# Retention units: outputs moved to the step of a later unit's scores, units 3.67 instead of 3.75 steps apart

## The chip, the cores and the metric

The kernel runs on one NeuronCore of a Trainium2 chip. The metric is the device time of one execution in microseconds (us); lower is better. The engines are named as in the profile: PE is TensorE (PEld its weight loads), DVE is VectorE, ACT is ScalarE, POOL is GpSimd, SP is SyncE, whose queue issues nearly all DMAs.

## What is computed

Retention (attention without softmax, with a decay per head), then a feed-forward layer with the gate h·cos(h), then a second one that takes the maximum of three projections:

```python
scores = scale * np.matmul(q, k.transpose(0, 1, 3, 2))      # 8 batches, 8 heads, 576 positions, 64 features
gamma = 1.0 - 2.0 ** (-5.0 - np.arange(H))
Dmat = np.where(rel >= 0, gamma[:, None, None] ** rel[None], 0.0)
attn_out = np.matmul(scores * Dmat[None], v)
x = attn_out.transpose(0, 2, 1, 3).reshape(B * S, H * D)    # 4608 tokens, 512 features
h = x @ w_in                                                # 512 -> 2048
x = (h * np.cos(h)) @ w_out                                 # 2048 -> 512
h = np.maximum(np.maximum(x @ w1, x @ w2), x @ w3)          # 512 -> 768
out = h @ w_out2                                            # 768 -> 512
```

All of it is in fp32. In the feed-forward layers each operand is split into a high and a low fp32r part, and the matrices are multiplied with seven quarter products (a Strassen-like scheme) instead of eight.

## The kernel before

The 4608 tokens are nine blocks of 512. Retention works in **units**: one unit is one block and one pair of heads, so there are 36 units; unit n is pair n % 4 of block n // 4, and its tile in the order of the instructions is named u{block}_{pair} (unit 18 is u4_2, its scores are sc18, its outputs po18). A unit goes through these functions:

- `att_load` (L550): one DMA of 1 MB on SP brings q, k and v of the unit into a tile of the pool `wpool` (8 buffers, shared with weights and with arenas in which weights are split).
- `att_scale` (L562): POOL scales v by the decay, in place.
- `att_scores` (L570): PE computes the scores of four chunks of 128 tokens, for two heads, into two PSUM banks. Contraction is over 64 rows, so a matmul uses a tile of 64 rows by 128 columns of the array.
- `att_mask` (L580): DVE multiplies the scores by the causal mask into SBUF.
- `att_state` (L609) and `att_keep` (L594): chunk by chunk, PE adds k·v to the running state of the head pair (128 by 128; 64 by 128 for a chunk of 64 tokens), which stands in one PSUM bank, and ACT copies the state before each chunk.
- `att_out` (L630): PE computes the outputs into one PSUM bank: masked scores times v (L637, 128 by 64 tiles), then the kept states times q (L649, 64 by 64 tiles).
- `att_decay` (L653): DVE scales the outputs into the block's quarters of x.

From these quarters `build_in` (L741) makes the split operands of the first feed-forward layer (differences on POOL, high parts on ACT, low parts on DVE) and SP stores them. The first layer's products for the first half of w_in run on PE in the same stretch (`group_in`, L458; `product_in`, L403): 12 matmuls of 256 columns per product on full 128 by 128 tiles, 14 products per block of tokens. The copies out of PSUM (L464, L470, the seed copy L487) and the gate (L516 to L540) are ACT's and DVE's, and SP stores the gate's results. `background` (L237) brings in later weights: a raw load (L180) on SP, a widening on ACT (L186), a join on DVE (L192), a sum on POOL (L198).

The order of work is written by hand. There is a list of **steps**; a product ends with `tick()` (L155), which runs what is due in that step. `at(k, fn, turn)` puts fn into the step k from now. Within a step, what is marked `AHEAD` comes first (scores and outputs, so they stand on PE between two products), `INSIDE` (state updates) goes into the next product or behind it, and the rest comes last. Every engine runs its own instructions in the order in which they were written. The first eight units run ahead of the products; from unit 8 on the start of a unit, in steps, is

```python
    def start_of(n):
        return (15 * (n - NLEAD)) // 4
```

and `att_unit` (L673) puts scores at the start, the mask one step later, the state updates in steps 1 to 5, the outputs in step 5 and the decay in step 6. The load is written four steps ahead of the start.

Of the kernel before, what the change touches and what calls it, by code (L numbers as in the profile page):

```python
# [39 lines left out]
def chunks_of(j):  # L40

    t0 = j * NB
    cut = (-t0) % S
    segs = [(0, cut), (cut, NB)] if 0 < cut < NB else [(0, NB)]
    out = [(a, min(CH, e - a)) for s, e in segs for a in range(s, e, CH)]
    full = [c for c in out if c[1] == CH]
    short = [c for c in out if c[1] < CH]  # L50
    assert len(short) in (0, 2) and all(n == CH // 2 for _, n in short)
    order = full + short
    col = {a: sum(n for _, n in order[:i]) for i, (a, _) in enumerate(order)}
    return [(a, n, col[a], (t0 + a) % S) for a, n in out]
# [47 lines left out]
def retention_ffn(ctx: ExitStack, tc: tile.TileContext, att, w_in, w_out, w123, w_out2, cst, out):  # L102
# [13 lines left out]
    def x4(name, shape, dt=F32):  # L116
        return xpool.tile([128, *shape], dt, tag="x", name=name)

    def bank(name):
        return ps.tile([128, NB], F32, tag="b", name=name)  # L120
# [21 lines left out]
    AHEAD, INSIDE, AFTER, LATER = range(4)  # L142

    def at(n, fn, turn=LATER):
        agenda.setdefault(slot[0] + n, [[], [], [], []])[turn].append(fn)
# [401 lines left out]
    def order_of(n):  # L547
        return divmod(n, NPAIR)

    def att_load(n):  # L550
        j, hp = order_of(n)
        w = w14(f"u{j}_{hp}", F32)
        units[n] = {
            "qk": w[:, : 2 * NB].rearrange("p (a n) -> p a n", a=2),
            "kv": w[:, 2 * NB : 4 * NB].rearrange("p (a n) -> p a n", a=2),
            "ret": w[:, 4 * NB : 6 * NB].rearrange("p (a n) -> p a n", a=2),
            "um": w[:, 6 * NB :].rearrange("p (k n) -> p k n", n=CH),
            "kept": {},
        }
        nc.sync.dma_start(out=w[:, : 4 * NB], in_=att[j, hp])  # L560

    def att_scale(n):  # L562

        v = units[n]["kv"][:, 1].rearrange("p (s d) -> p s d", d=64)
        col = CTV + n * 8
        nc.gpsimd.tensor_tensor(
            out=v, in0=v, in1=cs[:, col : col + 8].unsqueeze(2).to_broadcast([128, 8, 64]), op=ALU.mult
        )

    def att_scores(n):  # L570
        u = units[n]
        qT, kT = u["qk"][:, 0], u["qk"][:, 1]
        u["sc"] = [bank(f"sc{n}_{e}") for e in range(2)]
        for s in range(NB // CH):
            sl = slice(s * CH, (s + 1) * CH)
            for e in range(2):
                r = slice(64 * e, 64 * e + 64)
                nc.tensor.matmul(u["sc"][e][:, sl], kT[r, sl], qT[r, sl], start=True, stop=True)  # L578

    def att_mask(n):  # L580
        u = units[n]
        nfull = sum(m == CH for _, m, _, _ in chunks_of(order_of(n)[0]))
        for e in range(2):
            for at_, k, col in ((0, nfull, CM), (nfull, NB // CH - nfull, CM2)):
                if k:
                    sl = slice(at_ * CH, (at_ + k) * CH)
                    nc.vector.tensor_tensor(  # L587
                        out=u["ret"][:, e, sl].rearrange("p (s i) -> p s i", i=CH),
                        in0=u["sc"][e][:, sl].rearrange("p (s i) -> p s i", i=CH),
                        in1=cs[:, col : col + CH].unsqueeze(1).to_broadcast([128, k, CH]),  # L590
                        op=ALU.mult,
                    )

    def att_keep(n, i):  # L594

        u = units[n]
        j, hp = order_of(n)
        ch = chunks_of(j)
        if i >= len(ch):
            return  # L600
        _, m, _, pos = ch[i]
        st = state[:, hp * CH : (hp + 1) * CH]
        if pos:
            um = u["kept"][i] = u["um"][:, len(u["kept"])]
            nc.scalar.copy(um, st)  # L605
        if pos + m == S:
            nc.scalar.activation(st, cs[:, CM : CM + CH], AF.Copy, scale=0.0)

    def att_state(n, i):  # L609

        u = units[n]
        j, hp = order_of(n)
        ch = chunks_of(j)
        if i >= len(ch):
            return
        kn, v = u["kv"][:, 0], u["kv"][:, 1]
        _, m, c, pos = ch[i]
        if pos + m < S:
            s, p = divmod(c, CH)
            sl = slice(s * CH, (s + 1) * CH)  # L620
            nc.tensor.matmul(  # L621
                state[:, hp * CH : (hp + 1) * CH],
                kn[p : p + m, sl],
                v[p : p + m, sl],
                start=False,
                stop=True,
                skip_group_check=True,
            )

    def att_out(n):  # L630
        u = units[n]
        j, hp = order_of(n)
        qT, v = u["qk"][:, 0], u["kv"][:, 1]
        po = u["po"] = bank(f"po{n}")
        for s in range(NB // CH):
            for e in range(2):
                nc.tensor.matmul(  # L637
                    po[64 * e : 64 * e + 64, s * CH : (s + 1) * CH],
                    v[:, s * CH + 64 * e : s * CH + 64 * e + 64],
                    u["ret"][:, e, s * CH : (s + 1) * CH],  # L640
                    start=s == 0,
                    stop=False,
                    skip_group_check=True,
                )
        for i, um in u["kept"].items():
            _, m, c, _ = chunks_of(j)[i]
            for e in range(2):
                r = slice(64 * e, 64 * e + 64)
                nc.tensor.matmul(  # L649
                    po[r, c : c + m], um[r, r], qT[r, c : c + m], start=False, stop=True, skip_group_check=True  # L650
                )

    def att_decay(n):  # L653
        u = units.pop(n)
        j, hp = order_of(n)
        o = quarters_of.setdefault(j, {"name": f"x{j}", "n": NB})
        half = f"k{hp // 2 + 1}"
        if half not in o:
            o[half] = x4(f"{half}_x{j}", [2, NB])
        for _, m, c, pos in chunks_of(j):  # L660
            t, cc = divmod(c, HB)
            g = CGS + hp * 9 + pos // 64
            at_ = (hp % 2) * HB + cc
            nc.vector.scalar_tensor_tensor(
                out=o[half][:, t, at_ : at_ + m],
                in0=u["po"][:, c : c + m],
                scalar=cs[:, g : g + 1],
                in1=cs[:, CG + hp * CH : CG + hp * CH + m],
                op0=ALU.mult,
                op1=ALU.mult,  # L670
            )

    def att_unit(n, start):  # L673

        at(max(0, start - 1), lambda: att_scale(n))
        at(start, lambda: att_scores(n), AHEAD)
        at(start, lambda: att_keep(n, 0), AFTER)
        at(start + 1, lambda: att_mask(n))
        for i in range(5):
            at(start + i + 1, lambda i=i: att_state(n, i), INSIDE)  # L680
            if i < 4:
                at(start + i + 1, lambda i=i: att_keep(n, i + 1), AFTER)
        at(start + 5, lambda: att_out(n), AHEAD)
        at(start + 6, lambda: att_decay(n))

    NUNIT = NBLK * NPAIR

# [71 lines left out]
    NLEAD = 8  # L759
# [9 lines left out]
    for n in range(NLEAD):  # L769
        att_unit(n, 2 * n + 1)  # L770
# [5 lines left out]


    def start_of(n):
        return (15 * (n - NLEAD)) // 4

    for n in range(NLEAD, NUNIT):
        if n >= NLEAD + 2:
            at(max(0, start_of(n) - 4), lambda n=n: att_load(n))
        att_unit(n, start_of(n))
    per = 14
    for j in range(1, NBLK):
        build_in(block_of(j), per * j, (-11, -4, -3, -1), (-10, -8, -3, -1, 1, 1, 4), xsd[j], nc.gpsimd)
# [32 lines left out]
    for i in range(4):  # L820
        n = endA + (10, 38, 66, 90)[i]
# [763 lines left out]
```

## Time and profile before

| | |
|---|---|
| median of 3 runs | 1420.85 us (1419.0 to 1421.91) |
| the profiled execution | 1416.45 us |
| its span in the profile | 1413.9 us |
| PE busy | 1386.4 us (98%) |
| PEld busy | 1191.6 us (84%) |
| DVE, ACT, POOL busy | 1129.1, 812.6, 185.4 us |
| granted TensorE clock, mean | 0.995 |

How to read it: an engine's busy time is a mean over stages with different limits, so the stages are looked at one by one. Retention and the first half of the first layer's products fill the time from about 60 to 327 us; the rest of the first layer, w_out and the second layer follow. In a timeline the start of one piece of work less the start of the piece before is what the earlier piece cost on its engine. Ends of matmuls are modelled, so differences of starts are used, except for the release of a waiting DMA.

### The profile page before, as it was taken

How to read it: one execution, taken by the hardware profiler on the slowest of the kernel's cores; microseconds unless marked ns; L12 is line 12 of the kernel's file. 1: busy time of each engine (PE TensorE's matmuls, PEld its weight loads, DVE VectorE, ACT ScalarE, POOL GpSimd, SP SyncE). 2: the span in 40 equal slices, each digit the busy share in tenths (PEclk: the TensorE clock that was granted, in tenths of full speed). 3: DMA queues.
4: the chain of work that ended last, by engine and by line, in shares of the span. 5: the costliest groups of instructions: out<-in, count | busy, mean ns of one | idle time of the engine just before them, and what ended most of it. 6: DMA issues, size and time to landing. Idle time of an engine off the chain costs nothing.

```text
span 1413.9 us, 22274 instructions
## 1 busy us (share of the span) xinstructions
PE 1386.4 (98%) x8476; PEld 1191.6 (84%) x8476; DVE 1129.1 (80%) x1532; ACT 812.6 (57%) x1322; POOL 185.4 (13%) x148
## 2 busy tenths in 40 slices
PE   7999999999999989999999999999999999999998
PEld 5899999998888778888898888889888888888887
DVE  7978888789677779989879999578687567868885
ACT  4666666567687767756545656444454344544543
POOL 3333443331001000000011110110010000000000
PEclk8999999999999999999999999999999999999999
DMA  9679988887989977555568987534434486344733
GB/s 370 240 281 318 315 310 311 305 310 265 412 317 352 333 252 252 213 223 205 196 237 228 296 236 221 137 114 177 171 112 142 138 331 226 110 153 167 232 105 120
DMA packets 112939, 333.37 MB, mean 236 GB/s; under 512 B 9920, under 2 KB 18112, under 8 KB 107200
## 3 DMA queue, kind: packets, MB, share of 16 engines
q1 hardware_dynamic: 109952, 322.51, 63.8%
q0 software_dynamic: 2880, 9.44, 3.7%
q8 instruction: 66, 1.08, 0.3%
q14 instruction: 41, 0.34, 0.1%
HBM read 194.02 MB, written 137.89 MB: 235 GB/s over the span
## 4 chain that ended last, share of the span: by engine, by line
PE 84%; DVE 7%; ACT 4%; DMA 3%; issue 2%; POOL 0%; SPq 0%; DVEq 0%; ACTq 0%; POOLq 0%
PE d_e L439 14%; PE d_g L928 11%; PE b_e L439 7%; PE d_a L417 7%; PE b_g L928 6%; PE d_u L1446 5%; PE d_a L439 4%; PE a_e L439 3%; PE b_a L439 3%; PE b_a L417 3%; PE a_g L928 3%; PE b_u L1446 2%; PE po L637 2%; PE sc L578 2%; PE d_b L417 2%; PE sums L417 2%
## 5 line engine op out<-in xcount | busy, mean ns | idle before, releaser
L928 PE MATMUL d_g<-h_g,w_wo 128*128 128x512 f32 x512 | 157.9, 390 | 0.0
L464 ACT ACTIVATE ext<-d_e 128x512 f32<-128x512 f32 x72 | 43.1, 599 | 145.3 <-PE d_e L439 145.3
L895 DVE TENSOR_TENSOR l_g<-q_g,h_g 128x1024 fp32r<-128x1024 f32 x96 | 116.8, 1230 | 8.3 <-ACT h_g L888 7.7
L417 PE MATMUL d_a<-x_x,w_wi 128*128 128x256 f32 x864 | 122.5, 290 | 0.4 <-DVE x_x L394 0.2
L534 DVE SCALAR_TENSOR_TENSOR s_a<-t_a,s_a 128x1024 f32<-128x1024 f32 x68 | 91.1, 1340 | 32.3 <-ACT t_a L531 32.3
L888 ACT CAST h_g<-q_g 128x1024 fp32r<-128x1024 f32 x96 | 98.7, 1050 | 31.0 <-DVE q_g L879 20.0
L417 PEld LDWEIGHTS d_a<-x_x,w_wi 128*128 128x128 f32 x864 | 108.3, 191 | 6.1 <-issue 1.7
L928 PEld LDWEIGHTS d_g<-h_g,w_wo 128*128 128x128 f32 x512 | 96.0, 188 | 19.6
L928 PE MATMUL d_g<-l_g,w_wo 128*128 128x512 f32 x256 | 100.0, 391 | 0.6 <-DVE l_g L895 0.6
L525 DVE SCALAR_TENSOR_TENSOR t_a<-s_a,t_a 128x1024 f32<-128x1024 f32 x68 | 87.4, 1285 | 15.5 <-ACT t_a L521 15.4
L531 ACT ACTIVATE t_a<-t_a 128x1024 f32<-128x1024 f32 x68 | 71.9, 1058 | 37.4 <-DVE t_a L525 37.3
L439 PE MATMUL d_a<-y,w_wi 128*128 128x512 f32 x384 | 90.0, 390 | 2.1 <-ACT s_a L1052 1.4
L439 PEld LDWEIGHTS d_a<-y,w_wi 128*128 128x128 f32 x384 | 71.8, 188 | 17.7 <-ACT s_a L1052 1.8
L605 ACT COPY u<-state 128x128 f32<-128x128 f32 x128 | 31.4, 264 | 94.1 <-PE state L621 93.6
L521 ACT ACTIVATE t_a<-s_a 128x1024 int32<-128x1024 f32 x68 | 71.9, 1058 | 18.6 <-DVE s_a L1055 12.4
L439 PE MATMUL d_e<-h_e,w_b 128*128 128x512 f32 x304 | 81.5, 390 | 0.0
L928 PE MATMUL b_g<-h_g,w_wo 128*128 128x512 f32 x256 | 78.9, 390 | 0.0
L468 DVE TENSOR_TENSOR ext<-ext,b_e 128x512 f32<-128x512 f32 x36 | 24.7, 686 | 60.3 <-PE b_e L439 52.6
L439 PE MATMUL b_a<-y,w_wi 128*128 128x512 f32 x288 | 68.3, 392 | 1.1 <-ACT b_a L1061 1.1
L439 PEld LDWEIGHTS d_e<-h_e,w_b 128*128 128x128 f32 x304 | 56.9, 188 | 12.0 <-DVE ext L468 0.3
L439 PEld LDWEIGHTS b_a<-y,w_wi 128*128 128x128 f32 x288 | 53.6, 188 | 14.0 <-ACT b_a L1061 2.2
L417 PE MATMUL b_a<-x_x,w_wi 128*128 128x256 f32 x432 | 61.2, 290 | 1.2 <-DVE u L587 1.2
(376 smaller groups left out, 3466.0 us busy)
## 6 DMA issues: line engine op xcount, KB each, us to landing
u<-att SPq DMA_DIRECT2D x36, 1024.0 KB, 7.3
gqp<-s_a SPq DMA_DIRECT2D x64, 512.0 KB, 5.6
q_g<-gqp SPq DMA_DIRECT2D x64, 512.0 KB, 6.6
xsp<-x_x SPq DMA_DIRECT2D x56, 512.0 KB, 6.4
y<-xsp SPq DMA_DIRECT2D x56, 512.0 KB, 7.8
mqp<-ext SPq DMA_DIRECT2D x24, 512.0 KB, 3.7
st_b<-p_b SPq DMA_DIRECT2D x21, 512.0 KB, 6.4
w_b<-st_b SPq DMA_DIRECT2D x5, 1792.0 KB, 12.0
```

The costliest lines, as they stand in the source:

```text
L417: nc.tensor.matmul(h[:, p * HB : (p + 1) * HB], a, b, start=first and p == 0 and i == 0, stop=i == len(terms) - 1, skip_group_check=True,)
L439: nc.tensor.matmul(dst, a, b, start=first and i == 0, stop=i == len(terms) - 1, skip_group_check=True)
L464: nc.scalar.activation(dst, b[:, :n], AF.Copy, scale=scale)
L521: nc.scalar.activation(st["t"], s, AF.Copy, bias=0.25)
L525: nc.vector.scalar_tensor_tensor(out=r, in0=s, scalar=MOST_TURNS, in1=st["t"], op0=ALU.min, op1=ALU.subtract)
L531: nc.scalar.activation(r, r, AF.Sin, scale=TURN, bias=HALF_PI)
L534: nc.vector.scalar_tensor_tensor(out=s, in0=f32(st["t"]), scalar=-1.0, in1=s, op0=ALU.max, op1=ALU.mult)
L605: nc.scalar.copy(um, st)
L888: nc.scalar.copy(h, ts[i][q])
L895: nc.vector.tensor_tensor(out=lo, in0=t, in1=f32(h), op=ALU.subtract)
L928: nc.tensor.matmul(to, a, v[:, p].rearrange("p (b n) -> p b n", b=2) if half and n == 2 else v[:, :, r], start=first and k == 0 and p == 0 ...
L1446: nc.tensor.matmul(dst, a, v, start=first and p == 0 and i == 0 and (wide or mt == 0), stop=p == 2 and i == 2, skip_group_check=True,)
```

## The change

The outputs of a unit are no longer in the fifth step behind its scores but in the step in which the unit after the next has its scores, at the earliest in the fifth; the decay follows one step later. Units start 11/3 instead of 15/4 steps apart. The last two units, and the eight that run ahead of the products, keep their outputs in step 5.

```diff
-    def att_unit(n, start):
+    def att_unit(n, start, out_at=5):
...
-        at(start + 5, lambda: att_out(n), AHEAD)
-        at(start + 6, lambda: att_decay(n))
+        at(start + out_at, lambda: att_out(n), AHEAD)
+        at(start + out_at + 1, lambda: att_decay(n))
...
     def start_of(n):
-        return (15 * (n - NLEAD)) // 4
+        return (11 * (n - NLEAD)) // 3
...
-        att_unit(n, start_of(n))
+        att_unit(n, start_of(n), max(start_of(n + 2) - start_of(n), 5) if n + 2 < NUNIT else 5)
```

The outputs of unit n are entered into that step's list before the scores of unit n + 2, so they stand ahead of them. On PE before, from the outputs of unit 16 to the product behind the scores of unit 18 (po16 and sc18 are PSUM banks, u4_0 to u4_2 the tiles of units 16 to 18; the L417 rows are products, the L621 rows state updates):

```order
L637 MATMUL po16_1704<-u4_0_1429 64x128 x8
L649 MATMUL po16_1704<-u4_0_1429 64x128 x6
L417 MATMUL sums_137<-x_x2_1_1398,w_wi2_520 128x256 x6
L417 MATMUL sums_137<-x_x2_1_1398,w_wi3_683 128x256 x6
L621 MATMUL state_134<-u4_1_1521 128x128
L417 MATMUL d_a2_1_1664<-x_x2_4_1476,w_wi2_520 128x256 x6
L417 MATMUL d_a2_1_1664<-x_x2_4_1476,w_wi3_683 128x256 x6
L621 MATMUL state_134<-u4_1_1521 128x128
L578 MATMUL sc18_0_1763<-u4_2_1656 128x128
...
L417 MATMUL d_a2_0_1435<-x_x2_2_1623,w_wi0_209 128x256 x6
```

And with the change, on PE, from the last scores of unit 17 to the first of unit 18:

```order
L578 MATMUL sc17_1_1645<-u4_1_1528 128x128
L417 MATMUL d_a2_1_1660<-x_x2_0_1184,w_wi2_520 128x256 x6
L417 MATMUL d_a2_1_1660<-x_x2_0_1184,w_wi3_683 128x256 x6
L621 MATMUL state_134<-u4_1_1528 128x128
L417 MATMUL b_a2_1_1689<-x_x2_3_1235,w_wi2_520 128x256 x6
L417 MATMUL b_a2_1_1689<-x_x2_3_1235,w_wi3_683 128x256 x6
L417 MATMUL sums_137<-x_x2_1_1406,w_wi2_520 128x256 x6
L417 MATMUL sums_137<-x_x2_1_1406,w_wi3_683 128x256 x6
L621 MATMUL state_134<-u4_1_1528 128x128
L637 MATMUL po16_1727<-u4_0_1403 64x128 x8
L649 MATMUL po16_1727<-u4_0_1403 64x128 x6
L578 MATMUL sc18_0_1742<-u4_2_1601 128x128
```

Two products and two state updates stood between the outputs of unit 16 and the scores of unit 18; now nothing does, and three products stand between the scores of units 17 and 18.

On SP's queue before, around the load of unit 18 (xsp are stores of split operands, gqp stores of gate results):

```order
L751 DMA xsp0_72<-x_x2_4_1476 128x2x512
L751 DMA xsp0_72<-x_x2_6_1523 128x2x512
L751 DMA xsp0_72<-x_x2_5_1525 128x2x512
L560 DMA u4_2_1656<-att 128x2048
L540 DMA gqp0_1_81<-s0_a1_1_1233 128x2x512
L751 DMA xsp0_72<-x_x2_2_1623 128x2x512
```

And with the change, on SP:

```order
L751 DMA xsp0_72<-x_x2_4_1459 128x2x512
L560 DMA u4_2_1601<-att 128x2048
L751 DMA xsp0_72<-x_x2_6_1530 128x2x512
L751 DMA xsp0_72<-x_x2_5_1532 128x2x512
L540 DMA gqp0_1_81<-s0_a1_1_1233 128x2x512
L751 DMA xsp0_72<-x_x2_2_1605 128x2x512
```

Two stores that stood ahead of the load now stand behind it. In both kernels this load waits until the outputs of unit 15 have read the tile that it overwrites.

## Rows read from the trace of the kernel before

**Rows 1.** The page: busy time of each engine.
```profile
PE 1386.4 (98%) x8476; PEld 1191.6 (84%) x8476; DVE 1129.1 (80%) x1532; ACT 812.6 (57%) x1322; POOL 185.4 (13%) x148
```

**Rows 2.** Stages: us, busy PE, PEld, DVE, ACT, POOL, granted clock, DMA share, GB/s.
```profile
55.00:320.00 265.00, 264.46 (x2688) 242.56 (x2687) 219.29 (x386) 167.75 (x339) 103.74 (x71) 1.00 0.86 303
320.00:340.00 20.00, 18.29 (x164) 17.41 (x164) 17.99 (x31) 13.47 (x23) 4.79 (x3) 1.00 0.55 194
340.00:440.00 100.00, 98.75 (x501) 84.45 (x501) 75.26 (x102) 74.30 (x115) 7.76 (x6) 1.00 0.96 365
```

**Rows 3.** Waits of PE and PEld, 55 to 330 us: total, times, longest.
```profile
PE state L621 <- ACT u L605: 0.3, 1, 0.3
...
PEld state L621 <- ACT u L605: 0.5, 1, 0.5
```

**Rows 4.** Timeline of PE, 132 to 149 us: start, us, instruction.
```profile
133.64 0.88 PE L649 MATMUL po<-u 64*64 64x128 f32 x16
134.46 1.70 PE L417 MATMUL b_a<-x_x,w_wi 128*128 128x256 f32 x12
135.99 1.60 PE L417 MATMUL d_a<-x_x,w_wi 128*128 128x256 f32 x12
137.43 0.39 PE L621 MATMUL state<-u 128*128 128x128 f32 x2
...
140.74 1.68 PE L417 MATMUL b_a<-x_x,w_wi 128*128 128x256 f32 x12
142.35 1.09 PE L637 MATMUL po<-u 128*64 128x128 f32 x16
...
144.18 1.69 PE L417 MATMUL sums<-x_x,w_wi 128*128 128x256 f32 x12
145.71 0.39 PE L621 MATMUL state<-u 128*128 128x128 f32 x2
145.85 1.68 PE L417 MATMUL d_a<-x_x,w_wi 128*128 128x256 f32 x12
147.37 0.39 PE L621 MATMUL state<-u 128*128 128x128 f32 x2
147.68 1.16 PE L578 MATMUL sc<-u 64*128 64x128 f32 x16
148.78 1.70 PE L417 MATMUL d_a<-x_x,w_wi 128*128 128x256 f32 x12
```

**Rows 5.** SP's queue: waits 55 to 330 us, and its timeline at unit 18's load.
```profile
SPq L560 <- PE po L649: 56.1, 19, 6.8
...
134.60 0.35 SPq L560 DMA_DIRECT2D u<-att  x1
```

**Rows 6.** Landing of the unit loads: all 26 from 60 us; at 191.76; at 144.88.
```profile
DMA to landing us min/median/max: 5.2/7.0/9.5
...
DMA to landing us min/median/max: 5.2/5.2/5.2
...
DMA to landing us min/median/max: 9.5/9.5/9.5
```

**Rows 7.** Groups on PE, 55 to 320 us: busy us, mean ns, idle before.
```profile
L578 PE MATMUL sc<-u 64*128 64x128 f32 x432 | 31.4, 285 | 0.0
...
L621 PE MATMUL state<-u 64*128 64x128 f32 x26 | 6.3, 323 | 0.0
```

**Rows 8.** POOL's waits for unit loads, 58 to 330 us: total, times, longest.
```profile
POOL u L566 <- DMA u<-att: 48.0, 10, 7.0
```

**Rows 9.** Outputs of unit 21 on PE, and their scaled copy on DVE.
```profile
190.80 0.89 PE L649 MATMUL po<-u 64*64 64x128 f32 x16
...
194.45 1.24 DVE L664 SCALAR_TENSOR_TENSOR k_x<-po,cs 128x128 f32<-128x128 f32 x5
```

**Rows 10.** PE's wait for the seed copies, 320 to 560 us: total, times, longest.
```profile
PE sums L417 <- ACT sums L487: 2.8, 2, 1.6
```

**Rows 11.** Chain that ended last: the next stage's first matmuls.
```profile
356.78 2.75 PE d_a L439 x12
```

## The prediction

> **What bounds the kernel now.** I read the stages first [rows 1, 2]. TensorE (PE) is busy 98% of the span, and in the stretch that the change touches, 55 to 320 us, for 264.5 of 265 us at a granted clock of 1.00 (2.4 GHz); VectorE (DVE) has 219 us there, ScalarE (ACT) 168, GpSimd (POOL) 104. Next, who PE waits for in that stretch: the longest wait is 0.3 us, and 0.5 on its weight loads [rows 3]. So in that stretch the time is the length of PE's own list, and only what shortens that list, or makes PE wait, can move it.
>
> The third view is PE's timeline around units 15 to 18 [rows 4]. Read it by differences of starts. An input product of 12 matmuls takes 1.44 us behind another product (135.99 to 137.43), 1.53 behind a retention block (134.46 to 135.99) and 1.52 behind a state update (145.85 to 147.37). A state update takes 0.14 us before a product (145.71 to 145.85), but 0.31 before scores (147.37 to 147.68). Scores take 1.10 (147.68 to 148.78), outputs 1.83 (142.35 to 144.18). What differs is the form of the tile: products and full state updates use 128 rows by 128 columns, scores 64 by 128, the first part of the outputs 128 by 64, their second part 64 by 64. **A change of form costs time**: the entry 0.31 - 0.14 = 0.17 us behind a state update, and the return 1.53 - 1.52 = 0.01; or 1.61 (140.74 to 142.35) - 1.52 = 0.09 behind a product, where the return adds another 1.53 - 1.44 = 0.09. Either way a separate visit costs 0.18 us.
>
> Last, what a later place of the outputs could delay. A unit's load waits for the outputs of three units before: 19 of SyncE's (SP) load waits end there, 56 us in total [rows 5]. For unit 18 the outputs of unit 15 end at 133.64 + 0.88 = 134.52, its load is issued at 134.60, and its scores start at 147.68: 13.1 us for a load that lands in 7.0 us at the median, 9.5 at most [rows 4 to 6].
>
> **The change, part by part.**
>
> *Joined blocks.* For 26 units (8 to 33) the outputs move to the step of the scores of the next unit but one, ahead of them on PE. In the order of PE's matmuls changes of form fall from 173 to 147 over the phase: 27 places where outputs run into scores, one before. Gain: 26 x 0.18 = **4.7 us**. Bounds: the removed visit costs the same 0.18 by both rows above; if the step from 64x64 to 64x128 inside a joined block should be dearer than the return it replaces by as much as an entry behind a product (0.09), 2.3 us is left; nothing there could raise it above 26 x 0.31 = 8.1. I take 0.18, since the one neighbouring change inside a block, 128x64 to 64x64, is in every unit already, within its 1.83.
>
> A rule that would price this lower: PEld, the weight loads, is busy 242.6 of the same 265 us [rows 2], and each unit makes five changes of form; 27 units' scores are in the stretch (432 matmul records at 16 a unit) [rows 7], 135 changes, with the 13 short state updates (26 records at two each), in and out, 161. Their share of the 22.4 us without a weight load is 0.14 us each, or 26 x 0.14 = 3.6 us. The Trainium skill, Perfetto Trace Analysis, section Identifying the Most-Contended Engine, says that headroom on TensorE is read from weight-load time and not from matmul time; by it one would take 3.6 where the timeline gives 4.7. I keep 4.7, as the timeline shows the visit itself.
>
> *Closer spacing.* 3.67 steps instead of 3.75 moves the last unit's outputs from step 106 to 104. No instruction is added or removed, the number of products is fixed, PE is full there: 0 us by itself. Its cover is PE's full list; if a load comes late, the closer spacing makes that worse, which is counted next.
>
> *Loads.* The wait on the outputs three units back stays, but those now end directly before the scores of unit n-1 begin. For unit 18 the pieces between issue and scores are then: scores of 17 (1.10), products 1.53, 1.52 and 1.44, state updates 0.14 and 0.31, outputs of 16 (1.83), less 0.14 from the start of the block to the issue: **7.73 us** instead of 13.08. Counted so for every unit from 10 on, four have 7.73 (12, 18, 21, 27), two 8.32 (15, 24), two 8.55 (30, 33) and the other eighteen 9.39 to 10.2. With landings spread as before (read load by load, 8 of the 26 take over 7.73) I get about 1.3 us of PE wait in all. But SP now stands longer before each load with nothing else to issue. The load at 191.76, 4.3 us behind the last issue, landed in 5.2 us; the one at 144.88, 0.5 us behind another, in 9.5 [rows 6]. So most should land in 5 to 6.5 us. Bounds 0 and 1.3; I take **0.4**.
>
> *Queued behind the waiting load.* SP's stores of split inputs and gate results and the loads of raw weights stand behind it, up to 2.6 us longer (in a third of the units the load's turn is one step ahead of its release). Their waiters are ACT and DVE steps that need a buffer, and ACT's widening, three steps behind its raw load. POOL's scaling of v already stands waiting for loads, 48 us in ten waits [rows 8]; what follows on POOL has three steps to its reader. Cover: these steps; if gone, PE loses what ACT is late. 0 taken, bound 1.
>
> *State updates.* With outputs and scores no longer between them, 37 instead of 24 state updates stand one product behind the copy of the state that precedes them. PE waited 0.3 us for that copy in the whole stretch, its weight loads 0.5 [rows 3]; 13/24 of both is 0.4. I take **0.3**, bounds 0 and 0.8.
>
> *PSUM.* A joined block needs three banks in one step, so by the order some outputs take a bank that an earlier unit's outputs left only 3.1 to 3.8 us before, in PE's pieces [rows 4]; DVE's scaled copy out of it must end in that time. Unit 21's copy, the latest I saw, ended 4.0 us behind its outputs (190.80 + 0.89 to 194.45 + 1.24) [rows 9]. **0.3** taken, bounds 0 and 0.9 (one late copy in each block of tokens).
>
> **Sum.** 4.7 - 0.4 - 0.3 - 0.3 = 3.7 us less in that stretch. Behind it nothing is tied to a fixed time: PE's waits there, such as 2.8 us on two seed copies [rows 10], are on ACT and DVE, which work on PE's results, so they shift along; 3.7 reaches the end. The profiled execution was 1416.45 us (span 1413.9 and 2.5 around it), 4.4 below the median of the three runs; taken from it the sum gives 1412.75, and from the median 1420.85, which is what is forecast, **1417.1 us**.
>
> **Rivals.**
> 1. *The gain is taken back.* DVE is busy 18.0 of 20 us from 320 to 340, and the DMA engines 96% of the time from 340 to 440 [rows 2]. If DVE's backlog there has its own end, or transfers pace the next stage, PE comes earlier only to wait; the same result if a visit costs only the lower bound (2.3 less 1.0). For: PE's 2.8 us on seed copies [rows 10]. Against: PE is full again from 350 to 440 although the DMA engines are that busy. About 1.3 us left: 1419.5.
> 2. *Loads come late: slower.* The eight units with 7.73 to 8.55 us wait if their loads land later. It decides at about 8.6 us: 4 x 0.9 + 2 x 0.3 + 2 x 0.1 = 4.4 us of waits, against the 4.1 that the gain is without them. If all land in 9.5, the longest seen, it is 4 x 1.8 + 2 x 1.2 + 2 x 1.0 = 11.6, so 11.6 - 3.7 - 0.4 = 7.5 slower: 1428. For: the DMA engines are busy 86% in this stretch, and stores released in a burst follow each load. Against: 18 of 26 loads landed in under 7.73, and fewer will have traffic ahead. The Trainium skill, DMA: Bandwidth & Descriptors, section Anatomy of one DMA — SWDGE (gpsimd) path, has a DMA's wait stand on the issuing sequencer before dispatch; by it everything behind a waiting load on SP stands too, as the rows of SP show.
> 3. *The joined block is no cheaper*, that is, the change to 64x128 costs as much as a fresh visit (0.18 more): nothing gained, 1.0 lost to waits, 1422.
> 4. *More than counted*: the seed waits of 2.8 us vanish as the last units end two steps earlier: 1414.3.
>
> **Numbers.** About 0.2% (2.8 us) is what a measurement of this kernel can tell from no change. The forecast has a chance of 0.48, rival 4 0.08: faster 0.56. Rival 1 has 0.25 and rival 3 0.07: same 0.32. Rival 2 has 0.12. The range runs from 1413.5 (rival 4 less the scatter between runs, about 1) to 1423 (rival 3 and the mild part of rival 2), leaving out the late loads' tail. The forecast's own range is 1415 to 1418.
>
> **What would show it.** Right: outputs and scores as one block of 2.9 us 26 times; PE's waits for u's loads under 1 us in total; loads landing in under 7 us at the median; the next stage's first 512-column matmul, at 356.78 us now [rows 11], 3.7 us earlier. Wrong: PE waits on unit loads in several of units 12, 18, 21 and 27; a gap between the outputs' last matmul and the first score over 0.25 us; or that matmul not earlier by over 2 us.

## The result, and the profile after

The changed kernel takes **1432.4 us** (median of 6 runs, 1428.9 to 1436.6) against 1419.4 for the kernel before, run beside it: ratio 1.0096, 95% interval 1.0077 to 1.0116. It is 0.96% slower, where 1417.1 had been forecast and 1423 was the upper end of the range. The profiled execution took 1434.39 us (span 1432.6), 17.9 more than the one profiled of the kernel before, where the medians lie 13.0 apart: the shares below are those of this pair of executions.

The stages of the changed kernel, columns as in [rows 2]:

```profile
55.00:320.00 265.00, 247.72 (x2516) 228.31 (x2515) 207.98 (x358) 154.11 (x315) 96.67 (x68) 0.99 0.83 285
320.00:340.00 20.00, 20.00 (x190) 18.79 (x189) 18.59 (x34) 12.65 (x27) 5.03 (x4) 0.91 0.66 241
340.00:440.00 100.00, 96.94 (x567) 84.98 (x567) 75.96 (x106) 75.80 (x119) 11.13 (x7) 1.00 0.90 337
```

PE was full from 55 to 320 us; now it is busy for 247.7 of 265 us. The chain that ended last tells whether the loss was made up later:

```profile
374.96 2.75 PE d_a L439 x12
```

Its place before was 356.78 [rows 11]: 18.2 us later here, and the span is 18.7 longer. So the whole loss of this execution arises in the stretch of the change and passes on to the end undiminished.

Who PE and its weight loads wait for from 55 to 330 us (total, times, longest), to be read against [rows 3]:

```profile
PE state L621 <- ACT u L605: 15.1, 8, 3.1
PE sc L578 <- DMA u<-att: 1.4, 2, 0.9
...
PEld state L621 <- ACT u L605: 13.5, 7, 3.0
```

The unit loads, which the prediction feared, cost 1.4 us. The waits are those of state updates for ACT's copy of the state. ACT in the same stretch:

```profile
ACT ar_wo L186 <- DMA ar_wo<-w_out: 19.6, 4, 5.7
ACT ar_wi L186 <- DMA ar_wi<-w_in: 16.3, 6, 4.7
```

ACT stands ten times, 35.9 us in all, at the widening of a raw weight load that has not landed; in the kernel before it never did. The queue that issues those loads is SP's, and POOL stands at unit loads too ([rows 5, 8] before):

```profile
SPq L560 <- PE po L649: 133.6, 23, 11.6
...
SPq L180 <- DMA wf_wo<-ar_wo: 12.1, 2, 6.7
SPq L180 <- DMA wf_wi<-ar_wi: 7.2, 1, 7.2
...
POOL u L566 <- DMA u<-att: 116.6, 21, 10.4
```

SP stands 133.6 us at the unit loads where it stood 56.1, and what is written behind goes out with the 1 MB load or right after it. SP does not stand longer in all: its waits from 55 to 330 us add up to 217.0 us before and 211.1 with the change. They have moved from the stores to the unit loads. The stores' largest waits, two lines from before and one from after:

```profile
SPq L751 <- DVE x_x L394: 84.4, 31, 6.6
SPq L540 <- DVE s_a L534: 39.2, 21, 5.9
...
SPq L751 <- DVE x_x L394: 26.4, 6, 10.3
```

One case, from the timelines of SP, ACT and PE of the changed kernel (start, duration, instruction, in brackets the idle time before it and its releaser):

```profile
107.60 0.89 PE L649 MATMUL po<-u 64*64 64x128 f32 x16
...
108.62 0.35 SPq L560 DMA_DIRECT2D u<-att  x1
109.07 1.05 SPq L751 DMA_DIRECT2D xsp<-x_x  x2
110.22 1.02 SPq L180 DMA_DIRECT2D ar_wi<-w_in  x1
...
119.34 0.66 ACT L186 ACTIVATE ar_wi<-ar_wi 128x512 f32<-128x512 f32 x1 [4.74 <-DMA ar_wi<-w_in]
119.90 0.66 ACT L187 ACTIVATE ar_wi<-ar_wi 128x512 uint32<-128x512 uint32 x1
120.47 1.04 ACT L521 ACTIVATE t_a<-s_a 128x1024 int32<-128x1024 f32 x1
121.42 0.41 ACT L605 COPY u<-state 128x128 f32<-128x128 f32 x2
...
121.87 0.49 PE L621 MATMUL state<-u 128*128 128x128 f32 x2 [2.78 <-ACT u L605]
```

The outputs end at 107.60 + 0.89 = 108.49, and only then SP issues the unit load, two stores and the raw load. That lands 9.1 us later; ACT stands 4.74 us, does three steps, and only then the copy for which PE has been idle for 2.78 us. The raw loads of w_in from 60 to 320 us, before and after (the last figure is the median time from issue to landing):

```profile
ar_wi<-w_in SPq DMA_DIRECT2D x7, 512.0 KB, 4.9
...
ar_wi<-w_in SPq DMA_DIRECT2D x7, 512.0 KB, 9.1
```

Read load by load for the thirteen halves that ACT widens in this stretch, the lateness divides about evenly. The mean time from a raw load's issue to the moment when ACT is free to widen it falls from 8.7 to 5.7 us, and the mean landing grows from 5.2 to 8.0 us. A mean margin of 3.5 us has become a lack of 2.3.

A second loss hangs on the first. The granted clock, in windows of 4 us around three of the stalls (columns as in [rows 2]):

```profile
122.00:126.00 4.00, 4.00 (x19) 3.66 (x20) 4.00 (x10) 2.03 (x5) 2.64 (x2) 0.57 0.64 253
...
160.00:164.00 4.00, 4.00 (x40) 3.34 (x42) 2.57 (x6) 1.32 (x2) 4.00 (x3) 0.60 0.09 32
...
318.00:322.00 4.00, 2.16 (x12) 2.19 (x13) 3.54 (x4) 2.92 (x7) 2.59 (x2) 0.78 0.83 337
322.00:326.00 4.00, 4.00 (x28) 3.99 (x28) 4.00 (x9) 2.72 (x7) 1.73 (x2) 0.80 0.06 20
```

Here PE worked part of the time at half speed (1.2 instead of 2.4 GHz). The missing shares make 1.7 + 1.6 + 0.9 + 0.8 = 5.0 us; PE was idle in none of the time at half speed.

**The account.** From the first score of unit 9 to the first 512-column matmul (L439), I summed over PE's matmul records the idle time and, where the next matmul stands in another line of the code, the time from start to start without the idle part ("changes": here the cost of a change of tile form shows).

| kernel | ratio to before, 95% | stretch, us | idle | changes |
|---|---|---|---|---|
| before | 1 | 296.9 | 3.5 | 43.4 |
| the change | 1.0096 (1.0077 to 1.0116) | 315.0 | 20.3 | 40.8 |
| r3: joined at 3.75 | 1.0066 (1.0054 to 1.0078) | 305.9 | 12.1 | 40.0 |
| r4: spacing alone | 1.0002 (0.9994 to 1.0011) | 296.9 | 3.5 | 43.5 |
| r1: both raws, 5 and 9 | 1.0004 (0.9995 to 1.0013) | 295.9 | 6.4 | 39.1 |
| r2: before with r1's edit | 0.9999 (0.9990 to 1.0007) | 296.9 | 3.5 | 43.4 |
| r6: both raws, 4 and 8 | 0.9992 (0.9983 to 1.0000) | 295.4 | 6.1 | 39.3 |
| r9: both raws, 5 and 8 | 0.9989 (0.9980 to 0.9997) | 295.1 | 6.3 | 39.0 |
| r8: as r1, not joined | 0.9992 (0.9984 to 1.0001) | 295.9 | 3.1 | 43.3 |

The change: 16.8 us more idle, some 5 of slower matmuls, 4.3 less for changes of form (r1's figure; its own 40.8 holds slowed ones): 17.5 of the 18.1 us by which the stretch is longer.

### The profile page after: what moved, and what is told of

It reads as the page before. It is cut to its first block, busy times and chain, and to the rows that moved or that the text cites. A ratio compares the mean times of both kernels' runs of the same rounds, so it can differ in the third digit from the quotient of the medians.

```text
span 1432.6 us, 22271 instructions
## 1 busy us (share of the span) xinstructions
PE 1388.3 (97%) x8476; PEld 1195.2 (83%) x8476; DVE 1134.1 (79%) x1532; ACT 811.8 (57%) x1322; POOL 186.2 (13%) x148
## 4 chain that ended last, share of the span: by engine, by line
PE 63%; DVE 5%; ACT 3%; DMA 2%; issue 1%; SPq 0%; DVEq 0%; ACTq 0%
PE d_e L439 13%; PE d_g L928 11%; PE b_e L439 7%; PE b_g L928 6%; PE d_u L1446 5%; PE a_e L439 3%; PE a_g L928 3%; PE d_a L439 3%; PE b_u L1446 2%; PE b_a L439 2%; PE d_b L417 2%; DVE t_a L525 1%; PE a_u L1446 1%; PE d_gs L928 1%; PE b_b L417 1%
## 5 line engine op out<-in xcount | busy, mean ns | idle before, releaser
L417 PE MATMUL d_a<-x_x,w_wi 128*128 128x256 f32 x864 | 123.1, 293 | 0.1
L417 PEld LDWEIGHTS d_a<-x_x,w_wi 128*128 128x128 f32 x864 | 110.2, 194 | 3.4 <-DVE x_x L394 0.3
L525 DVE SCALAR_TENSOR_TENSOR t_a<-s_a,t_a 128x1024 f32<-128x1024 f32 x68 | 88.1, 1296 | 20.7 <-ACT t_a L521 20.5
L531 ACT ACTIVATE t_a<-t_a 128x1024 f32<-128x1024 f32 x68 | 72.0, 1059 | 35.9 <-DVE t_a L525 35.9
L439 PE MATMUL d_a<-y,w_wi 128*128 128x512 f32 x384 | 90.0, 390 | 2.0 <-ACT s_a L1052 1.4
L439 PEld LDWEIGHTS d_a<-y,w_wi 128*128 128x128 f32 x384 | 71.8, 188 | 17.6 <-ACT s_a L1052 1.8
L439 PE MATMUL d_e<-h_e,w_b 128*128 128x512 f32 x304 | 81.4, 390 | 0.2 <-DVE ext L468 0.2
L605 ACT COPY u<-state 128x128 f32<-128x128 f32 x128 | 31.2, 263 | 87.2 <-PE state L621 86.5
L439 PE MATMUL b_a<-y,w_wi 128*128 128x512 f32 x288 | 67.8, 390 | 1.1 <-ACT b_a L1061 1.1
L621 PE MATMUL state<-u 128*128 128x128 f32 (+1 forms) x256 | 52.8, 294 | 16.2 <-ACT u L605 15.5
L439 PEld LDWEIGHTS d_e<-h_e,w_b 128*128 128x128 f32 x304 | 56.9, 188 | 12.3 <-DVE ext L468 0.7
L566 POOL TENSOR_TENSOR u<-u,cs 128x512 f32<-128x512 f32 x36 | 47.4, 1317 | 150.7 <-DMA u<-att 128.7
```

The source lines that it names most:

```text
L417: nc.tensor.matmul(h[:, p * HB : (p + 1) * HB], a, b, start=first and p == 0 and i == 0, stop=i == len(terms) - 1, skip_group_check=True,)
L439: nc.tensor.matmul(dst, a, b, start=first and i == 0, stop=i == len(terms) - 1, skip_group_check=True)
L525: nc.vector.scalar_tensor_tensor(out=r, in0=s, scalar=MOST_TURNS, in1=st["t"], op0=ALU.min, op1=ALU.subtract)
L531: nc.scalar.activation(r, r, AF.Sin, scale=TURN, bias=HALF_PI)
L566: nc.gpsimd.tensor_tensor(out=v, in0=v, in1=cs[:, col : col + 8].unsqueeze(2).to_broadcast([128, 8, 64]), op=ALU.mult)
L621: nc.tensor.matmul(state[:, hp * CH : (hp + 1) * CH], kn[p : p + m, sl], v[p : p + m, sl], start=False, stop=True, skip_group_check=True,)
```

## The experiments

**r1 and r2: load both raw halves at once.** In the loop that places the background blocks of the first stage:

```diff
-        at(per * j + 1, lambda: background(*back.pop(0), True, 3))
+        at(per * j + 1, lambda: background(*back.pop(0), True, 5, True, 4))
```

The 3 was the number of steps from a load to its widening. Now both halves are loaded at once (`True`), the first is widened after 5 steps and the second 4 later. The steps of the second widening (9) and of the block's store (13) stay.

> Changed kernel, with both raw halves of a background block loaded at once and widened 5 and 9 steps later (instead of 3 steps after each load). Theory A (SP stands at the unit load longer, the raw load behind it lands late, ACT waits for it at L186 in front of the state copy L605, TensorE waits for the copy): ACT's waits at L186 between 55 and 330 us fall from 35.9 us to under 5, TensorE's waits for the copy of the state from 15.1 us to under 3, no granted clock of 0.5 after stalls in the stretch, and the gain of the joined blocks is left: 1414 to 1418 us, 1.5 to 5 us under the kernel before. Theory B (the closer spacing of the units, with loads and state copies that are short of time whatever the raw loads do): TensorE's waits for the copy stay at 10 us or more, 1427 to 1434 us. Theory C (TensorE's joined blocks cost the time themselves): waits at L186 gone and the time still over 1427 us. If 0.5 MB more in the burst makes the unit loads late, TensorE's waits for unit loads (1.4 us) grow over 8 us and the time lies near 1425 us.

Measured: 1417.5 us, ratio 1.0004. PE's waits from 55 to 330 us:

```profile
PE sc L578 <- DMA u<-att: 1.4, 2, 0.8
PE d_a L417 <- DVE x_x L394: 1.0, 1, 1.0
PE state L621 <- ACT u L605: 0.6, 2, 0.3
PE sums L417 <- DVE x_x L394: 0.3, 1, 0.3
```

ACT no longer waits at L186 at all. The loss of 13 us is gone, although SP still stands 128 us and POOL 100 us at the unit loads. The edit gives the raw loads more time, and they also land sooner (median 6.6 us for w_in against 9.1). r9 below tells the two apart: there they land no sooner than in the change (9.9 us), and ACT has no wait at L186 either, so more time is enough. Theory A's gain did not come: 1.5 to 5 us under the kernel before had been expected, and the median is 0.6 over it.

> Kernel before with the same edit of the raw loads (both halves at once, widened 5 and 9 steps later): a control of what that edit does by itself. Theory A: ACT had no wait at L186 there to lose, so no change: 1417 to 1422 us, with TensorE's waits between 55 and 330 us as before. If the edit is a gain of its own: under 1416 us, and then the first run says nothing of the joined blocks unless it is taken against this one.

Measured: 1417.5 us, ratio 0.9999. The edit is worth nothing by itself, so r1's cure is a cure of the change. The closer spacing and the joined blocks are all still in r1: theories B and C fall.

**r3 and r4: the two parts apart.** r3 is the change with `start_of` as before (and outputs joined up to unit 31, since a later one would come behind the reader of its block); r4 is the kernel before with

```diff
-        return (15 * (n - NLEAD)) // 4
+        return (11 * (n - NLEAD)) // 3
```

> The first part of the change alone: outputs joined to the scores of the next unit but one (units 8 to 31, 24 of the 26), units 3.75 steps apart as before. Theory A (late outputs hold the unit load, and so the raw load): SP's wait at the unit load for the outputs' product stays over 100 us, ACT waits at L186 for 20 to 36 us, TensorE waits for the copy of the state for 8 to 16 us, and the time is 1424 to 1434 us. Theory B (the closer spacing): the waits at L186 are under 5 us and the time is 1413 to 1418 us.

> The second part of the change alone: units 3.67 steps apart, outputs five steps after the scores as before. Theory A: SP's wait at the unit load stays near 56 us (under 80), ACT's waits at L186 under 5 us, TensorE's waits for the copy under 3 us, 1417 to 1422 us. Theory B: the waits at L186 or for the copy of the state as in the changed kernel (10 us or more), 1426 to 1434 us.

Measured: r3 1426.9 us, r4 1417.0. SP's wait at the unit loads in r3, then in r4:

```profile
SPq L560 <- PE po L649: 120.2, 22, 9.2
```

```profile
SPq L560 <- PE po L649: 64.6, 19, 6.2
```

Theory A holds in both: the late outputs make the loss, the spacing alone makes none. In r3 ACT waits 21.5 us at L186 and PE 7.4 us for ACT's state steps (4.8 of it in one wait for the clearing of the state, L607), a little under the 8 expected. Together the two parts cost more than the first alone (1.0096 against 1.0066); why, no run separates.

**r5: the wait without the change.** The kernel before, with each raw half widened one step behind its load instead of three.

> Kernel before (outputs not joined, 3.75 steps), with each raw half of the background blocks of the first stage widened one step after its load is issued instead of three: makes ACT's wait at L186 without anything of the change. Theory A (an ACT that waits for a raw load in front of the state copy is what costs): ACT's waits at L186 between 55 and 330 us go from 0 to 25 to 50 us in ten or more, TensorE's waits for the copy of the state from 0 to 8 to 20 us, the granted clock falls to 0.5 behind the longest of them, and the time is 1426 to 1440 us. Rival (ACT's waits are covered by the slack of the copy, and it is the late outputs that cost): ACT's waits appear, TensorE's waits for the copy stay under 3 us, 1416 to 1420 us.

Measured: 1419.5 us, ratio 1.0009 (0.9999 to 1.0019). ACT waits 12.1 us in seven at L186, less than I had expected, since SP issued these loads on average 6.1 us before ACT reached the widening. Only the longest reached PE; ACT first, then PE:

```profile
252.88 0.66 ACT L186 ACTIVATE ar_wo<-ar_wo 128x512 f32<-128x512 f32 x1 [4.10 <-DMA ar_wo<-w_out]
...
254.30 0.49 PE L621 MATMUL state<-u 128*128 128x128 f32 x2 [1.75 <-ACT u L605]
```

By its numbers the rival came out: PE waits 2.0 us for the copy, and the time is within the rival's. What the rival adds, that the late outputs cost by themselves, does not fit r1, whose outputs are as late and which loses nothing. So r5 shows the chain once in the kernel before, with a slack of about 2.4 us at that copy (4.10 - 1.75), and is too small a dose to price it. A slack of this size fits that ten waits of 35.9 us cost PE 15.1 us, but it differs from place to place: in the change a wait of ACT of 4.08 us, at 101.49, is followed by no wait of PE for the copy, and one of 1.46 us, at 157.09, by 1.86 us.

**r13: only the second half early.** Both halves loaded at once, widened at 3 and 9 as in the change (`True, 3, True, 6`).

> Changed kernel with both raw halves loaded at once, widened 3 and 9 steps later, just the steps of the changed kernel: the first half as short of time as in it, only the second half is loaded early. In the changed kernel ACT's waits at L186 were 14.8 us for first halves and 21.0 us for second halves. Theory A (the time between load and widening, each half by itself): the second halves' waits go, the first halves' 10 to 18 us stay, TensorE's waits for the copy of the state fall from 15.1 us to 4 to 9 us, and the time is 1421 to 1428 us, between the changed kernel and the run with 5 and 9 steps. Rival (loading the second half without waiting for GpSimd's sum of the first is the whole cure): the first halves' waits go too, under 4 us, 1416 to 1419 us.

Measured: 1418.4 us, ratio 0.9999 (0.9991 to 1.0008). The first halves' waits stay, 10.0 us in four, none over 3.3; but PE waits only 1.1 us for the copy:

```profile
ACT ar_wi L186 <- DMA ar_wi<-w_in: 7.7, 3, 3.3
...
ACT ar_wo L186 <- DMA ar_wo<-w_out: 2.3, 1, 2.3
```

Neither side came out whole: ACT's waits are theory A's, PE's and the time are the rival's. The cure lies in the second halves: in the change each of them is loaded only after POOL's sum of the first, three steps before its widening. The trace of the change agrees: of PE's seven waits over 1 us for the copy, five, 11.4 of 14.8 us, stand behind the widening of a second half. In r13 the second halves are asked for six steps earlier and need no sum; which of the two counts, it does not separate. The first halves' waits that are left stay within the copy's slack. (A wait of 2.9 us for a split input, at 238 us, where r1 has 1.0, makes up most of the 2.5 us by which r13's stretch is longer than r1's.)

**r10 and r11: one step more, loads one at a time.** r10 asks for every raw load one step earlier, r11 widens one step later; nothing else moves but, in r11, what follows the widening (join, sum and the block's store).

> Changed kernel, outputs joined and raw halves loaded one at a time as in it, each raw load only asked for one step (about 2.7 us) earlier and widened in the same step as in the changed kernel: a half dose of the cure. Theory A: ACT's waits at L186 fall from 35.9 us to 8 to 20 us, TensorE's waits for the copy of the state from 15.1 us to 1 to 7 us, and the time is 1418 to 1427 us, between the changed kernel and the first run. Rival (the cure lay in loading both halves in one place, not in the time between load and widening): ACT's waits stay over 25 us and the time over 1428 us.

Measured: 1425.5 us, ratio 1.0054 (1.0039 to 1.0070). ACT's waits fall to 9.3 us and PE's for the copy to 2.2, as theory A had it, but the raw loads, now often ahead of unit loads on SP, stand there for POOL's sum (30.0 us) and for the landing of earlier stores (23.0 us), and PE pays at the unit loads:

```profile
PE sc L578 <- DMA u<-att: 5.3, 3, 1.8
PE state L621 <- ACT u L605: 2.2, 3, 1.5
```

> Changed kernel with every raw load asked for in the same step as in it, one at a time, and only the widening (with what follows it) one step later: no load is moved on SP's queue but the block's store, which goes out a step later. Theory A: ACT's waits at L186 fall from 35.9 us to under 12 us and TensorE's waits for the copy of the state from 15.1 us to under 4 us; TensorE's waits for unit loads stay under 4 us (in the tenth run the raw loads were moved ahead of unit loads and these waits were 5.3 us): 1417 to 1424 us. Rival (the waits for ACT are replaced by waits for unit loads whatever is done): TensorE's waits for unit loads over 5 us, 1424 us and more.

Measured: 1429.6 us, ratio 1.0094 (1.0072 to 1.0115): a miss for both. The time is on the rival's side, but PE's waits for unit loads are 1.2 us and not over 5. The account gives a stretch of 310.6 us with 16.0 idle. ACT still waits 17.6 us, and one case shows the link that I had left out (SP, ACT, PE):

```profile
171.87 0.35 SPq L560 DMA_DIRECT2D u<-att  x1
172.31 0.39 SPq L300 DMA_DIRECT2D wf_wi<-ar_wi  x1
172.79 0.38 SPq L540 DMA_DIRECT2D gqp<-s_a  x1
181.29 0.33 SPq L180 DMA_DIRECT2D ar_wi<-w_in  x1
...
185.48 0.66 ACT L186 ACTIVATE ar_wi<-ar_wi 128x512 f32<-128x512 f32 x1 [7.12 <-DMA ar_wi<-w_in]
...
188.01 0.48 PE L621 MATMUL state<-u 64*128 64x128 f32 x2 [4.31 <-ACT u L605]
```

The store of a finished block goes out with the burst, and the next block's raw load needs that buffer: it is issued only at 181.29, 8.5 us behind the gate's store before it. SP stands 30.6 us for landings of such stores (19.3 in the change, 7.6 before). What r11 gives the widening it takes from the store. DVE's joins also moved, and PE waits 4.6 us more for split inputs (L394).

**r8: what the joining is worth.** r1 with outputs one step ahead of the scores, so the blocks are apart again:

```diff
-max(start_of(n + 2) - start_of(n), 5)
+max(start_of(n + 2) - start_of(n) - 1, 5)
```

> Changed kernel with both raw halves loaded at once (5 and 9 steps), and the outputs one step ahead of the scores of the next unit but one, so that the two blocks are not joined: what the joining alone is worth, against the first run. If a joined block saves 0.18 us at each of the 26 visits: TensorE's changes of tile form cost 4 to 5 us more than in the first run, its waits stay about the same or fall by up to 2 us, and the time is 2 to 5 us over the first run: 1419.5 to 1422.5 us. If joining saves nothing: the same as the first run, or less by the waits, 1415 to 1418 us.

Measured: 1417.3 us, ratio 0.9992. The changes of form cost 4.3 us more than in r1 (43.3 against 39.1), as expected; but r8's idle time is 3.4 us less than r1's, and both stretches take 295.9 us. Joining is real, and as late as it must be for that, it gives back nearly all of it in waits.

**r6, r7, r9, r12: looking for a version that keeps the gain.** All have both halves loaded at once as in r1. They are widened 4 and 8 steps later in r6, 5 and 8 in r9, 6 and 9 in r12; r7 is r1 with unit loads written three steps ahead instead of four.

> Changed kernel with both raw halves loaded at once, widened 4 and 8 steps later, so that the block's store goes out a step earlier than in the first run. In the first run two unit loads waited for such a store to land (8.3 us) and TensorE for those unit loads (1.4 us). Theory A: SP's wait at the unit load for that store falls under 3 us, TensorE's waits for unit loads under 0.5 us, ACT's waits at L186 stay under 3 us, and the time is 1 to 2 us under the first run's 1417.5: 1415 to 1417 us. If the store lands no earlier: 1417 to 1418 us.

> Changed kernel with both raw halves loaded at once (5 and 9 steps), and the unit load asked for one step later (three steps ahead of the unit's scores, not four), behind the step in which the outputs that free its buffer are made. If SP's standing at that load is what holds the other transfers: its wait for the outputs' product falls from 128 us to under 90 us, and unit loads land as late as before, since they are issued at the release: 1415 to 1418 us. If the load is then issued later than the release: TensorE's waits for unit loads grow from 1.4 us to over 4 us, 1419 to 1424 us.

> Changed kernel with both raw halves loaded at once, widened 5 and 8 steps later: the first half as late as in the first run of this edit (where ACT had no wait at L186), the second and the store a step earlier. Theory A: ACT's waits at L186 under 2 us, TensorE's waits for the copy of the state under 1 us; unit loads still wait now and then for a store's landing (8.3 us at 5 and 9 steps, 20.5 us at 4 and 8), since the late outputs leave no spare buffer, and TensorE for them by 0.5 to 2 us; the 4.2 us from the joined blocks less some 2.5 us of waits: 1415 to 1418 us, 0 to 2 us under the kernel before. If joined blocks come free of new waits: 1412.5 to 1414.5 us.

> Changed kernel with both raw halves loaded at once, widened 6 and 9 steps later (5 and 8 gave 1416.2 us, 0.9989 of the kernel before, 5 and 9 gave 1.0004). The steps at which ACT's widening meets the table load of the sines differ in each. If the wait of 1.4 us for the copy of the state at 80 us (ACT was at a widening and a table load) goes with the step: 1414 to 1416.5 us. If the store's landing is what decides (it is as late as at 5 and 9): 1416.5 to 1418.5 us.

Measured: r6 1416.8, r9 1416.2, r12 1417.2 us (ratio 1.0001, 0.9992 to 1.0010), r7 1422.2 (1.0035, 1.0021 to 1.0048). r9 is the lowest of the study, 0.1% under the kernel before: its interval just excludes no change, but it is the lowest of seven versions with both halves loaded at once, and the gain is less than the 0.2% that the prediction took for what one measurement can tell. So a gain is not safely shown. Its waits of PE (the profiled execution, 1422.0 us, was the slowest of its twelve):

```profile
PE state L621 <- ACT u L605: 1.9, 2, 1.4
PE sc L578 <- DMA u<-att: 0.9, 1, 0.9
PE d_a L417 <- DVE x_x L394: 0.5, 1, 0.5
```

The 1.4 us are behind a load of ACT's activation table, 1.28 us at 78.01, between a widening and the copy. In r6 the store's earlier step did not help: SP's waits at unit loads for store landings rose from 8.3 to 20.5 us. In r7 SP's wait for the outputs fell from 128 to 90 us as hoped, but it then stood at stores for DVE's split inputs instead (62.6 us against 25.9), and unit loads went out late (PE's waits 3.2 us, and 1.8 for one split input). In r12 the wait for the copy at 80 us is gone (0.6 us for the copy in all), and waits for unit loads (1.1 us) and a split input (1.0 us) stand in its place.

**r14: the state copy on DVE.** L605 `nc.vector.tensor_copy(um, st)` in place of `nc.scalar.copy(um, st)`.

> Changed kernel with the copy of the state before a unit's state updates (L605) made by VectorE instead of ScalarE, and nothing else changed: the raw loads land as late as in it. Theory A (it is the place of the copy behind the waiting widening that brings the wait to TensorE): ACT's waits at L186 stay over 25 us, and TensorE's waits for the copy fall from 15.1 us to under 6 us, since VectorE waits for the widening less (12.2 us at L191 in the changed kernel); VectorE carries 0.2 to 0.3 us more at each of some 100 copies, so that TensorE may wait for VectorE's operands instead: 1418 to 1428 us. Rival (the copy is late for another reason, such as the state's own updates): TensorE's waits for the copy stay over 10 us and the time over 1428 us.

Measured: 1471.3 us, ratio 1.0366 (1.0351 to 1.0381). DVE waits 45.4 us for state updates from 55 to 340 us, and PE 19.9 us for the copy: DVE, the fuller engine, made every copy later, in the first eight units too. With everything late the raw loads had time (ACT's largest wait for them 4.2 us). By the numbers (over 10 us for the copy, over 1428 us) it is the rival's side, but here it is DVE itself that makes the copy late, so r14 says nothing on the link that it was meant to cut.

## Why the prediction was wrong

- **What bounds the kernel** held: PE's list, and only what makes PE wait. So did the pass-through: 18.2 us of loss by the end of the stretch, 18.7 in the span.
- **Joined blocks**, 4.7 us: right, a little large. The account gives 4.1 to 4.4 less for changes in r1, r6, r9 and r12. In r1 a joined block reads

```profile
127.38 1.09 PE L637 MATMUL po<-u 128*64 128x128 f32 x16
128.40 0.89 PE L649 MATMUL po<-u 64*64 64x128 f32 x16
129.22 1.16 PE L578 MATMUL sc<-u 64*128 64x128 f32 x16
130.31 1.10 PE L417 MATMUL d_a<-x_x,w_wi 128*128 128x256 f32 x7
```

  128.40 to 129.22 is 0.82, what outputs took before a product as well (133.64 to 134.46 in [rows 4]): the step to the scores' form is not dearer, and rival 3 falls. The 3.6 us that the prediction set beside it, an estimate from PEld's busy time after the Trainium skill's advice to judge headroom by weight loads (Perfetto Trace Analysis, section Identifying the Most-Contended Engine), was too low by about as much as 4.7 was too high.
- **Closer spacing**, 0: right alone (r4). With late outputs the change is slower than r3 (1.0096 against 1.0066), as the prediction allowed for ("if a load comes late"), but with no price.
- **Loads**, 0.4 taken, bound 1.3: 1.4 us in two waits. But "most should land in 5 to 6.5 us" was wrong; the median is 7.5 us:

```profile
DMA to landing us min/median/max: 5.9/7.5/9.7
```

  I had looked at the traffic ahead of the load and not at what is released together with it. The two units that waited were 25 and 29, none of the four with the shortest time.
- **State updates**, 0.3, and **PSUM**, 0.3: the wait for the copy is 0.6 us in r1, where nothing else disturbs it, against 0.3 before, so the 0.3 fits. Neither r1 nor the change has a wait of PE for a bank that DVE's scaled copy had still to empty, so that 0.3 was not needed (r10 has one, of 1.4 us).
- **Queued behind the waiting load**: the step that failed. I named the waiter ("ACT's widening, three steps behind its raw load") and took 0, at most 1, on the cover of three steps, without looking up how much of the three steps was free. In the trace of before the raw loads' data lay ready 1.4 to 7.2 us before their widening began (thirteen halves, widened from 79.9 to 297.2 us), a margin of 3.5 us on average. The change took away 3.0 us of it before the issue and 2.8 in the landing, so it had to show. And "if gone, PE loses what ACT is late" I never carried through ACT's order: the state copy stands behind the widening, and PE behind the copy. In place of 0 it cost 15.1 us of waits for the copy in the profiled execution, and with the slower clock behind them some 20. The Trainium skill, DMA: Bandwidth & Descriptors, section Anatomy of one DMA — SWDGE (gpsimd) path, cited with rival 2, has a DMA's wait stand on the issuing sequencer; the section describes GpSimd's DMAs, and SP's 133.6 us at unit loads show the same for SP's. The prediction drew from it that what is behind stands too, and then priced the unit loads alone.
- **Rival 2**, slower by late loads, had the sign and the place in SP's queue, but the wrong transfer. **Rival 1**, the gain taken back, is what r1, r6, r9 and r12 show once the raw loads are cured, by waits in the same stretch rather than behind it.

Open: why the raw loads land more slowly in the change. That it is the traffic that goes out with them is argued and not shown alone; in r10, where they often stand ahead of the unit loads, thirteen halves land in 5.2 us on average, as before. Open too is which one change would remove the 3 us of scattered waits that the joined versions have more than r8.

## What to carry to other kernels

When an instruction is moved later and a queue waits for it, list everything behind it on that queue, and for each transfer compare its slack (landing to first use) with the extra delay; then follow the engine that uses it in its own order, for the step that comes late there may have nothing to do with the moved work. A saving of some 0.17 us a visit is real and can be read from start differences, but it has to be set against the waits that the later place brings: 4.3 us against 3.4 between r1 and r8. If a load's buffer is free early, ask for it early: loading both halves at once freed the second of POOL's sum of the first.

## What was not expected of the hardware

After three stalls the granted clock fell to its lower level (1.2 GHz) for some microseconds (windows above), which makes about 5 us of a loss of 18; the kernel before had none between 55 and 320 us. The length of the idle time does not tell which stall is followed by it: after idle times of 2.78, 1.86 and 3.08 us the clock fell, after 2.12 us (at 276.80) it did not, nor in r13 after 2.87 us at 238.72:

```profile
238.00:242.00 4.00, 3.28 (x30) 3.16 (x32) 3.45 (x5) 1.91 (x4) 0.12 (x1) 1.00 0.82 228
```
